# Moving the routing work, the first expert blocks and the first loads of a fused attention and expert kernel

## The chip, the cores and the metric

The kernel runs on one core of one Trainium2 chip. The metric is the device time of one execution in microseconds (us); smaller is better. A core has five engines that run side by side and wait for one another through semaphores: PE (matrix products, with PEld for its weight loads), DVE (vector), ACT (scalar functions), POOL (GpSimd) and SP (which here only issues transfers). Each engine works through its own list of instructions strictly in the order in which the program gives them. So the place of an instruction in the program text matters: what stands behind a waiting instruction on the same engine waits too.

## The reference

The first part is attention with random features. For each of 8 batches and 8 heads, with 576 rows of 64 values:

```python
proj = np.einsum('bhsd,md->bhsm', x, omega)                  # x is q or k; 128 features
phi = np.concatenate([np.cos(proj), np.sin(proj)], -1) / np.sqrt(m)
kv = np.einsum('bhsm,bhsd->bhmd', k_p, v);  z = np.sum(k_p, axis=2)
out = np.einsum('bhsm,bhmd->bhsd', q_p, kv) / np.einsum('bhsm,bhm->bhs', q_p, z)[..., None]
```

The heads of a row are put side by side: 4608 rows of 512 values. The second part sends each row to one of 8 experts:

```python
xn = x / (np.linalg.norm(x, axis=-1, keepdims=True) + 1e-06)  # en: the same of expert_emb
logits = xn @ en.T / tau;  expert_idx = np.argmax(logits, axis=1)
gate_w = softmax(logits)[np.arange(N), expert_idx]
out[mask] = gate_w[mask, None] * (np.maximum(x[mask] @ w1[e], 0) @ w2[e])   # mask: rows of expert e
```

## The kernel before

The attention runs in 32 steps; a step works on two heads of one batch. The steps are software-pipelined: step n makes the features of pair n, finishes pair n - 1 and prepares pair n + 1. One turn of the loop, cut to what is spoken of below (`nx` is true while another step follows):

```python
for n in range(NS + 1):                       # NS = 32; the turn n = NS finishes the last pair
    if n < NS - 2: load_v(n + 1)
    if n > 0: kv_copy(n - 1)                  # DVE
    if n > 1: to_rows(n - 2); sums(n - 2)     # POOL: rows to fp16, logits of the heads added up
    ...                                       # store_rows (SP), one 512 KB piece of expert weights (POOL)
    if n == NS - 1: gather(0)                 # POOL: 128 rows by index, the first expert block
    if n < NS:
        proj_q(n, ...)                        # PE, L233 and L241
        fold(n, "k"); whole_turns(n, "q"); wave(n, "si", "k")    # DVE, ACT, ACT
        zsum(n, 0)                            # POOL, L282 to L285
    route_first(n)                            # DVE: routing of the first two groups of batches
    if n == NS: turn_x(0, "act"); gather(3); hidden(0, "act")
    if n > 0:
        kv_turn(n - 1)                        # PE, L316 and L324; L324 reads the sums of zsum
        kv_out(n - 1)                         # DVE, L334: PSUM to the tile kv
    if nx: proj_k(n + 1); whole_turns(n + 1, "k")                # PE L221, ACT L254
    if n < NS: frac(n, "q"); wave(n, "co", "k"); zsum(n, 1)
    ...                                       # gather(1), square sums, frac(n + 1, "k")
    if n > 0: num(n - 1)                      # PE, L349, 72 matmuls; reads kv
    if n == NS: turn_x(1, "act")
    if n < NS: fold(n, "q")
    if nx: turns(n); copy_k(n); copy_q(n); load_kq(n + 1)        # PE L185
    route_pe(n)
    if n < NS: kv_products(n); wave(n, "si", "q"); wave(n, "co", "q")   # PE L295
    if n > 0: norm(n - 1)
    route_pool(n)                             # POOL: square roots of the norms, L724
    if n == NS - 1: gather(2)
```

The routing goes in two parts. The first covers groups 0 and 1 of the four groups of two batches and lies in the steps, so that 11 expert blocks can begin before the second part is known. The steps are counted from n0 = 10 and n1 = 18:

```python
elif n == n0 + 6: r1["g0"] = gates(0, 1, r1["rt", 0][0], ar1)     # step 16
elif n == n0 + 7: gates2(0, 1, *r1["g0"]); store_gates(0, 1)
m = n - n1
...
elif m == 2: scan(); square_rows(GRP1 - 1)                         # step 20
elif m == 8: row_hot(oh1, r1["lo"], 0, 6); choose(GRP1)            # step 26
elif m == 9: row_hot(oh1, r1["lo"], 6, 12); r1["g1"] = gates(1, 2, ...)
elif m == 10: row_hot(oh1, r1["lo"], 12, S1); block_experts(0, K1, False, r1["a"])
elif m == 12: gates2(1, 2, *r1["g1"]); store_gates(1, 2)
elif m == 13: square_rows(GRP1); choose2(GRP1)                     # step 31

def gates(g0, g1, rn, ar):                    # the weight of the chosen expert, first half
    nc.vector.tensor_tensor(sh, lsq[...], bc(lmax[...]), ALU.subtract)    # L732
    nc.vector.tensor_scalar(rn, rn, 1e-6, None, ALU.add)                  # L733; rn comes from POOL's root
    nc.vector.reciprocal(rn, rn)                                          # L734
    nc.vector.tensor_tensor(sh, sh, bc(rn, shp, 2), ALU.mult)             # L735
    nc.scalar.activation(sh, sh, AF.Tanh, scale=0.5)                      # L736, ACT
```

Then come the expert blocks of 128 rows, 40 that are always run and 3 behind a branch:

```python
def block(j, end):
    if j + 1 < end: hidden(j + 1, "act")      # PE L848, 32 matmuls; ACT
    route_second_pe(j)                        # rank at j = 2, invert at j = 7
    if j < end - 2: turn_x(j + 2, "act")      # PE L806 transposes; ACT copies
    route_second(j)                           # DVE; at j = 0 also root: POOL, 18 columns
    if j + 4 < NBLK: gather(j + 4)            # POOL
    result(j)                                 # PE L869, 8 matmuls; ACT; scatter of the rows (POOL, L886)
for j in range(LAST): block(j, LAST)          # LAST = 40
nb = nc.values_load(nblk[0:1, 0:1], ...)
with tc.If(nb > LAST): ...                    # the three further blocks
```

At the start the tile `kq` holds one pair's q and k; `load_kq(0)` comes after the transposes that free it.

Of the kernel before, what the change touches and what calls it, by code (L numbers as in the profile page):

```python
# [28 lines left out]
def kernel(  # L29
# [12 lines left out]
    nc = tc.nc  # L42
# [72 lines left out]
    eblk = persist.tile([1, NBLK], I32)  # L115
    nblk = persist.tile([1, 1], I32)
# [12 lines left out]
    pm = persist.tile([P, SG], FP32)  # L129
# [4 lines left out]
    with tc.tile_pool(name="psA", bufs=1, space=PSUM) as psA, tc.tile_pool(  # L134
# [5 lines left out]
        nm2 = ps[:, 6 * 512 :].rearrange("p (a w) -> p a w", a=2)  # L140

# [17 lines left out]
        ROUTED = tuple(range(n1 + 1, n1 + 13))  # L159


        def load_kq(m):
# [4 lines left out]
            t = pa.tile([P, 2 * NCH, 64], FP32, tag="kq", name="kq", bufs=1)  # L167
# [209 lines left out]
        def to_rows(n):  # L377
            b, i = steps[n]
            if i % 2 == 0:
                xrow[b, i // 2] = pa.tile([P, NCH, 2, 64], FP16, tag="xb", name="xb")  # L380
            nc.gpsimd.tensor_copy(xrow[b, i // 2][:, :, i % 2], st[n]["xa"][:, 0:NCH, 0:64])
# [18 lines left out]
        def square_rows(g):  # L400
            s0 = g * SG
            for par in range(2):
# [3 lines left out]
                nc.vector.tensor_copy(t[here, :, NPAIR:], t[there, :, 0:NPAIR])  # L406
                nc.vector.tensor_reduce(
# [3 lines left out]
        def sums(n):  # L411
            b, i = steps[n]
            src = st[n]["xa"][:, 0:NCH, 64 : 64 + E]
            if i == 0:
                lacc[b] = pa.tile([P, NCH, E], FP32, tag="la", name="la", bufs=3)
                nc.gpsimd.tensor_copy(lacc[b], src)
            else:
                nc.gpsimd.tensor_tensor(lacc[b], lacc[b], src, ALU.add)
# [25 lines left out]
        load_kq(-1)  # L444
        load_v(0)
        make_identity(nc, ident)
        nc.vector.memset(zmask, 0.0)
        nc.vector.memset(pio2, PI_2)
        nc.vector.memset(zmask[0:64, 0:1], 1.0)
# [47 lines left out]
        copy_k(-1)  # L497
        copy_q(-1)
        frac(0, "k")
        load_kq(0)  # L500
# [50 lines left out]
        def choose(g):  # L551
# [4 lines left out]
            nc.vector.tensor_copy(l0, a0[64:P])  # L556
            nc.vector.tensor_copy(l1, a1[0:64])
            nc.vector.tensor_tensor(l0, l0, a0[0:64], ALU.add)
            nc.vector.tensor_tensor(l1, l1, a1[64:P], ALU.add)
            nc.vector.tensor_reduce(lmax[:, s0 : s0 + SG], lg, axis=AX.X, op=ALU.max)  # L560

        def choose2(g):
# [3 lines left out]
            nc.vector.tensor_tensor(sel, lg, bc(mx, [P, SG, E], 2), ALU.is_equal)  # L566
            nc.vector.tensor_tensor(sel, sel, bc(pref, [P, SG, E], 1), ALU.mult)
            nc.vector.tensor_reduce(pm, sel, axis=AX.X, op=ALU.max)
            nc.vector.tensor_tensor(
# [9 lines left out]
        def scan():  # L579
            nc.vector.tensor_tensor_scan(flat(cumx), flat(keep), flat(eq), 0.0, ALU.mult, ALU.add)  # L580
# [9 lines left out]
        def before(dst, src, ar):  # L590

            t = ar.take(E * E).rearrange("p (a b) -> p a b", b=E)
            nc.vector.tensor_tensor(t, bc(src, [P, E, E], 1), tri, ALU.mult)
            nc.vector.tensor_reduce(dst.unsqueeze(2), t, axis=AX.X, op=ALU.add)

        def whole(dst, src, shift, mid=None):
            mid = dst if mid is None else mid
            nc.vector.tensor_scalar(mid, src, 1.0 / P, shift, ALU.mult, ALU.add)
            nc.vector.tensor_scalar(dst, mid, CMAGIC, CMAGIC, ALU.add, ALU.subtract)

        def starts1(rk, ns, ar):
            nc.vector.tensor_copy(sm[:, T0], rk[:, :, ns])
# [3 lines left out]
        def starts1b():  # L606
            nc.vector.tensor_scalar(sm[:, LIM], sm[:, FB], float(P), None, ALU.mult)
            nc.vector.tensor_scalar(sm[:, OFF1], sm[:, B1], float(P), None, ALU.mult)
            nc.vector.memset(sm[:, DOFF], BIG)

        def starts2(rk, ns, ar):
            nc.vector.tensor_copy(sm[:, T0], rk[:, :, ns])
            whole(sm[:, T1], sm[:, T0], 0.49609375)
            nc.vector.tensor_tensor(sm[:, T1], sm[:, T1], sm[:, FB], ALU.subtract)
            before(sm[:, ST2], sm[:, T1], ar)
            nb1 = sm[:, 8, 0:1]
            nc.vector.tensor_tensor(nb1, sm[:, B1, E - 1 : E], sm[:, FB, E - 1 : E], ALU.add)
            nc.vector.tensor_tensor(sm[:, ST2], sm[:, ST2], nb1.to_broadcast([P, E]), ALU.add)
            nc.vector.tensor_tensor(sm[:, T0], sm[:, ST2], sm[:, FB], ALU.subtract)
# [574 lines left out]
```

## Time and profile before

The median time is 497.8 us, of three executions from 496.01 to 497.95. The profiled execution spans 492.0 us.

| engine | busy us | share of the span |
|---|---|---|
| PE (matmuls) | 462.8 | 94% |
| PEld (weight loads) | 389.2 | 79% |
| POOL | 366.9 | 75% |
| ACT | 356.2 | 72% |
| DVE | 299.8 | 61% |

A line of the timeline gives the start and the duration in us, the engine, the line of the program, the operation and its tiles as out<-in, and in brackets how long the engine had stood idle and what ended that. A line of the chain of waits gives start, duration, engine, tile and line. The windows give, for a stretch of time, how long each engine was busy in it, the clock that PE was granted (1.00 is full) and the share of time in which the transfer engines worked.

### The profile page before, as it was taken

The page shows a single profiled execution, that of the slowest core. Times are in us where ns is not written, and L with a number is a line of the kernel's source. Part 1 is how long each engine was busy: PE and PEld are TensorE (multiplying, and loading weights), DVE is VectorE, ACT ScalarE, POOL GpSimd, SP SyncE. Part 2 cuts the span into 40 slices and gives each one's busy share as a digit, 9 for nine tenths or more (in the row PEclk, how much of TensorE's full clock was granted, in tenths as well). Part 3 has the DMA queues.
Part 4 walks back from the last instruction along what each step waited for, and adds up shares of the span by engine and source line. Part 5 has one row for each costly group of instructions (what it writes and reads, how often), then busy time and mean ns, then how long its engine had stood idle before and what let it go on. Part 6 is the DMA issues. An engine that isn't in the chain of part 4 may idle for free.

```text
span 492.0 us, 18747 instructions
## 1 busy us (share of the span) xinstructions
PE 462.8 (94%) x7924; PEld 389.2 (79%) x7924; DVE 299.8 (61%) x518; ACT 356.2 (72%) x473; POOL 366.9 (75%) x472
## 2 busy tenths in 40 slices
PE   8899999999999798999999999779999999999991
PEld 7788898898898687888888888566777777777770
DVE  4689888799888798898888788728930000000000
ACT  3787887887887587989887989725666666666661
POOL 3698888889899877889999788946765555554551
PEclk9999999999999899999998999989999999999997
DMA  4588798897777677977877779612433223232220
GB/s 123 143 175 161 182 169 166 184 172 158 182 157 153 133 146 185 161 163 159 173 140 161 167 152 170 101 41 68 120 104 103 97 88 106 82 119 89 83 81 20
DMA packets 57652, 65.63 MB, mean 133 GB/s; under 512 B 29397, under 2 KB 37589, under 8 KB 57568
## 3 DMA queue, kind: packets, MB, share of 16 engines
q0 software_dynamic: 18064, 30.96, 32.1%
q1 hardware_dynamic: 39104, 32.95, 26.6%
q8 instruction: 65, 1.06, 0.9%
q10 hardware_dynamic: 400, 0.49, 0.3%
q14 instruction: 19, 0.16, 0.1%
HBM read 67.90 MB, written 15.22 MB: 169 GB/s over the span
## 4 chain that ended last, share of the span: by engine, by line
PE 64%; POOL 13%; DVE 8%; DMA 5%; ACT 4%; issue 4%; SPq 1%; POOLq 0%; ACTq 0%; DVEq 0%
PE ps L848 13%; PE ps L869 12%; PE ps L349 12%; PE ps L295 8%; PE ps L185 5%; PE ps L221 4%; POOL zt L282 4%; PE ps L233 3%; POOL zs L284 2%; POOL zt L283 2%; POOL zs L285 2%; DMA kq<-in_k_dram 2%; PE ps L806 2%; PE ps L324 2%; DMA kq<-in_q_dram 1%
## 5 line engine op out<-in xcount | busy, mean ns | idle before, releaser
L349 PE MATMUL ps<-kv,siq 128*64 128x73 f32 x1152 | 79.4, 234 | 6.4 <-DVE kv L334 6.2
L848 PEld LDWEIGHTS <-w_sb 128*128 x1280 | 76.1, 99 | 10.6 <-issue 1.6
L848 PE MATMUL ps<-kq,w_sb 128*128 128x128 f16 x1280 | 79.3, 221 | 1.4 <-ACT kq L798 1.4
L349 PE MATMUL ps<-kv,coq 128*64 128x73 f32 x1152 | 77.9, 231 | 0.0
L869 PE MATMUL ps<-w_sb,cok 128*128 x320 | 75.4, 379 | 0.2 <-issue 0.2
L349 PEld LDWEIGHTS ps<-kv,siq 128*64 128x64 f32 x1152 | 64.0, 140 | 10.5 <-ACT sik L271 3.8
L349 PEld LDWEIGHTS ps<-kv,coq 128*64 128x64 f32 x1152 | 64.6, 141 | 0.0
L282 POOL TENSOR_TENSOR zt<-sik 128x512 f32<-128x512 f32 x32 | 41.0, 1281 | 25.2 <-ACT sik L271 25.0
L767 POOL DMA_INDIRECT xin_all<-rf_x,prm x43 | 45.7, 1062 | 15.4 <-PE ps L806 9.6
L869 PEld LDWEIGHTS <-cok 128*128 128x128 f16 x320 | 29.7, 98 | 28.9 <-issue 0.4
L283 POOL TENSOR_TENSOR zt<-zt 128x256 f32<-128x256 f32 x64 | 48.6, 759 | 5.0
L258 DVE SCALAR_TENSOR_TENSOR sik<-sik,ps 128x1152 f32<-128x1152 f32 x32 | 43.2, 1349 | 3.7 <-ACT sik L254 3.7
L208 ACT ACTIVATE qT<-ps 128x512 f32<-128x512 f32 x32 | 19.1, 596 | 35.6 <-DVE kT L199 35.6
L282 POOL TENSOR_TENSOR zt<-cok 128x512 f32<-128x512 f32 x32 | 43.9, 1373 | 0.8 <-ACT cok L271 0.8
L221 PE MATMUL ps<-omT,kT 64*128 64x128 f32 x576 | 44.0, 283 | 0.3 <-DVE kT L202 0.3
L258 DVE SCALAR_TENSOR_TENSOR siq<-siq,ps 128x1152 f32<-128x1152 f32 x32 | 43.0, 1344 | 1.8 <-ACT siq L254 1.8
L185 PE MATMUL ps<-ident,kq 128*128 128x128 f32 x288 | 38.4, 279 | 2.8 <-DMA kq<-in_k_dram 2.3
L295 PE MATMUL ps<-sik,v 64*64 64x128 f32 x612 | 37.4, 272 | 3.4 <-issue 3.4
L886 POOL DMA_INDIRECT out_dram<-siq,prm x20 | 22.3, 1117 | 23.6 <-ACT siq L885 22.3
L271 ACT ACTIVATE coq<-coq,consts 128x1152 f32<-128x1152 f32 x32 | 39.9, 1248 | 0.0
L271 ACT ACTIVATE cok<-cok,consts 128x1152 f32<-128x1152 f32 x32 | 39.9, 1248 | 0.0
L254 ACT ACTIVATE sik<-ps 128x1152 f32<-128x1152 f32 x32 | 36.2, 1132 | 4.8 <-PE ps L221 2.9
(213 smaller groups left out, 1158.9 us busy)
## 6 DMA issues: line engine op xcount, KB each, us to landing
w_sb<-in_moe_w_dram POOLq DMA_DIRECT2D x32, 512.0 KB, 6.6
kq<-in_q_dram SPq DMA_DIRECT2D x63, 144.0 KB, 3.7
kq<-in_k_dram SPq DMA_DIRECT2D x63, 144.0 KB, 3.9
v<-in_v_dram SPq DMA_DIRECT2D x34, 144.0 KB, 3.9
rf_x<-xb SPq DMA_DIRECT2D x32, 144.0 KB, 7.8
xin_all<-in_v_dram SPq DMA_DIRECT2D x30, 144.0 KB, 4.3
xin_all<-rf_x,prm POOLq DMA_INDIRECT x43, 2.9
out_dram<-sik,prm POOLq DMA_INDIRECT x20, 2.8
```

The source lines that it names most:

```text
L185: nc.tensor.transpose(qreg[:, j * P : j * P + P], t[:, j * P : j * P + P], ident)
L221: nc.tensor.matmul(kreg[:, s * P : s * P + P], lhsT=t[r0 : r0 + 64, j * P : j * P + P], rhs=omT[r0 : r0 + 64], start=True, stop=True,)
L254: nc.scalar.activation(si, REG[nm], AF.Copy, bias=CMAGIC, scale=1.0)
L258: nc.vector.scalar_tensor_tensor(out=si, in0=si, scalar=CMAGIC, in1=REG[nm], op0=ALU.subtract, op1=ALU.subtract)
L271: nc.scalar.activation(t, t, AF.Sin, bias=pio2 if which == "co" else 0.0, scale=-TWO_PI * SINSC)
L282: nc.gpsimd.tensor_tensor(zt, t[:, 0:4], t[:, 4:8], ALU.add)
L283: nc.gpsimd.tensor_tensor(zt[:, 0:2], zt[:, 0:2], zt[:, 2:4], ALU.add)
L295: nc.tensor.matmul(kreg[64 * half : 64 * half + 64, 512 * hh : 512 * hh + P], lhsT=d["v"][r0 : r0 + 64, c], rhs=ph[r0 : r0 + 64, s * P : s ...
L349: nc.tensor.matmul(nm2[r0 : r0 + 64, a, (c - c0) * W : (c - c0) * W + W], lhsT=ph[:, s * P + r0 : s * P + r0 + 64], rhs=d["kv"][:, half, h ...
L767: ins = nc.gpsimd.indirect_dma_start(out=t, out_offset=None, in_=x_rows[:], in_offset=bass.IndirectOffsetOnAxis(ap=prm[:, j : j + 1], axis=0),
L848: nc.tensor.matmul(h_ps[:, f * P : f * P + P], lhsT=weights(k), rhs=d["xT"][:, c * P : c * P + P], start=(c == 0), stop=(c == 3),)
L869: nc.tensor.matmul(y_ps, lhsT=d["hT"][:, c * P : c * P + P], rhs=weights(NW1 + NW2 * (j % 2) + c), start=(c == 0), stop=(c == NW2 - 1),)
```

## The change

It has six parts.

1. **Loads at once.** The q and k of the first pair get their own place (in the room of a late expert's weights), so the next pair's load need not wait. The order of the first copies is changed too, and each piece of expert weights is issued one step earlier from step 2 on.
2. **Gates once, in place.** The weights of groups 0 and 1 are computed together, in steps 24 to 30, in the tile that holds the logits; the computation in steps 16 and 17 goes.
3. **Routing work held.** The DVE instructions of `route_first` are kept back, let out up to an estimated 0.9 us before `kv_out`, and the rest behind it; in the last step all of it comes behind.
4. **First block woven into the last step.** `turn_x(0)` moves ahead of the last `kv_products`, and the gathers 1 to 3 behind the sums on POOL. Rows of two late steps are converted on ACT.
5. **Second routing.** The rank is taken at block 1, the inversion at block 6; the roots move to blocks 3 and 4 in pieces, the gates to block 5.
6. **Last scatters.** The scatters of blocks 38 and 39 stand behind the branch.

The diff, cut to its core (`...` marks the cuts; `nc.vector` became `rv` throughout the routing helpers):

```diff
+        held = []
+        hold = [False]
+        def do(f, *a, **k):
+            if hold[0]:
+                held.append((f, a, k))
+            else:
+                f(*a, **k)
...
+        rv, ra = Engine(nc.vector), Engine(nc.scalar)
+        def release(budget):
+            spent = 0.0
+            while held:
+                ...                             # width: elements of the output in a partition
+                cost = 0.2 + width / 960.0
+                if spent + cost / 2 > budget:
+                    return
+                spent += cost
+                held.pop(0)
+                f(*a, **k)
...
-            t = pa.tile([P, 2 * NCH, 64], FP32, tag="kq", name="kq", bufs=1)
+            if m == -1:
+                t = (w2_sb[:, E - 2] ... )
+            else:
+                t = pa.tile([P, 2 * NCH, 64], FP32, tag="kq", name="kq", bufs=1)
...
         load_kq(-1)
+        load_kq(0)
         load_v(0)
...
         turns(-1)
-        copy_k(-1)
         copy_q(-1)
         frac(0, "k")
-        load_kq(0)
+        fold(0, "k")
+        copy_k(-1)
...
+            if NS - 3 <= n < NS - 1:            # in to_rows
+                nc.scalar.activation(dst, src, AF.Copy)
+            else:
+                nc.gpsimd.tensor_copy(dst, src)
...
-        def gates(g0, g1, rn, ar):
...
+        def gates_a(g0, g1):
+            rv.tensor_tensor(sh, sh, bc(lmax[:, s0:s1], shp, 2), ALU.subtract)
+        def gates_b(g0, g1):
+            rv.tensor_scalar(rn, rn, 1e-6, None, ALU.add)
+            rv.reciprocal(rn, rn)
+            rv.tensor_tensor(sh, sh, bc(rn, [P, s1 - s0, E], 2), ALU.mult)
+            ra.activation(sh, sh, AF.Tanh, scale=0.5)
+        def gates_c(g0, g1):                    # 1 - sh, reciprocal
+        def gates_d(g0, g1):                    # sum, times 2, minus E, reciprocal
...
-            elif n == n0 + 6:
-                r1["g0"] = gates(0, 1, r1["rt", 0][0], ar1)
-            elif n == n0 + 7:
-                gates2(0, 1, *r1["g0"])
-                store_gates(0, 1)
...                                             # gates_a at m == 6
             elif m == 8:
                 row_hot(oh1, r1["lo"], 0, 6)
-                choose(GRP1)
+                gates_b(0, GRP1)
...                                             # gates_c at m == 11
             elif m == 12:
-                gates2(1, 2, *r1["g1"])
-                store_gates(1, 2)
+                gates_d(0, GRP1)
+                store_gates(0, GRP1)
+                choose(GRP1)
...
-        WORDER = [None, 0, 1, *range(2, 4 * E - 4), ...]
+        WORDER = [*range(4 * E - 4), ...]
...
-            for piece in () if n == 0 else WORDER[n + 1 : n + 2] if n > 1 else WORDER[1:3]:
+            for piece in () if n == 0 else WORDER[n + 1 : n + 2] if n > 2 else WORDER[2 * n - 2 : 2 * n]:
...
+            hold[0] = True
             route_first(n)
+            hold[0] = False
+            release(0.9 if n < NS - 1 else 0.0)
             if n == NS:
-                turn_x(0, "act")
-                gather(3)
                 hidden(0, "act")
             if n > 0:
                 kv_turn(n - 1)
                 kv_out(n - 1)
+            release(100.0)
...
-            if n == NS:
-                turn_x(1, "act")
+            if n >= NS - 1:
+                turn_x(n + 1 - NS, "act")
...
             if n == NS - 1:
+                gather(1)
                 gather(2)
+                gather(3)
...
-            if j == 2:
-                r2["ps"] = rank(NSLOT, bank(6))
-            elif j == 7:
+            if j == 1:
+                r2["ps"] = rank(NSLOT, bank(6 - 4 * (j % 2)))
+            elif j == 6:
                 r2["inv"] = invert(
...
-                root(GRP1, *r2["rt"], 0, (NGRP - GRP1) * SG)        # block 0
...
+            if j in (3, 4):                     # block
+                for a in range(GRP1 * SG + SG * (j - 3), GRP1 * SG + SG * (j - 2), 3):
+                    root(a, a + 3)
             result(j)
+            if not LAST - 2 <= j < LAST:
+                scatter(j)
...
+        scatter(LAST - 2)
+        scatter(LAST - 1)
```

## The prediction

> **What bounds the kernel now.** I read the page first, then the chain of waits, PE's list of waits, and the timeline at each place where the chain leaves PE. PE is busy for 94% of the span, and it leads the chain:
>
> ```profile
> PE 462.8 (94%) x7924; PEld 389.2 (79%) x7924; DVE 299.8 (61%) x518; ACT 356.2 (72%) x473; POOL 366.9 (75%) x472
> ...
> 41.48 1.31 PE ps L221 x18
> ...
> 50.71 1.31 PE ps L221 x18
> ...
> 344.89 1.79 PE ps L848 x32
> 346.90 1.73 PE ps L869 x8
> 348.62 1.79 PE ps L848 x32
> ```
>
> The lines below the first are of the chain. Two `proj_k` (L221) start 50.71 - 41.48 = 9.23 us apart, and two blocks 348.62 - 344.89 = 3.73. In both stretches PE works without a gap, and the change takes no matmul away. So only what a step takes beyond 9.23 us, a block beyond 3.73, and the two ends can be won. From PE's timeline, the starts of `proj_q` (L233) show which steps are long: step 16 takes 13.72 us (159.64 to 173.36; 4.49 too many), 18 takes 10.92 (1.69), 20 takes 9.92 (0.69), 21 9.48 (0.25), 26 11.99 (2.76), 28 10.21 (0.98). The other small ones add 1.9: 12.7 us in all. PE's own waits name the releasers (total, times, longest):
>
> ```profile
> PE ps L349 <- DVE kv L334: 6.2, 6, 2.6
> PE ps L295 <- issue: 3.4, 1, 3.4
> PE ps L185 <- DMA kq<-in_k_dram: 2.3, 2, 1.6
> PE ps L324 <- POOL zs L285: 1.7, 5, 0.9
> PE ps L848 <- ACT kq L798: 1.4, 2, 0.7
> ```
>
> The first is `num` waiting for `kv_out` while DVE still does routing. The timelines of DVE and PE in step 16 and in step 31:
>
> ```profile
> 162.72 0.63 DVE L733 TENSOR_SCALAR w_sb<-w_sb 128x9 f32<-128x9 f32 x1 [1.31 <-POOL w_sb L724]
> ...
> 163.64 2.08 DVE L735 TENSOR_TENSOR w_sb<-w_sb 128x72 f32<-128x72 f32 x1
> 165.64 0.45 DVE L334 COPY kv<-ps 128x292 f32<-128x292 f32 x1
> ...
> 166.24 0.51 PE L349 MATMUL ps<-kv,siq 128*64 128x73 f32 x4 [2.63 <-DVE kv L334]
> ...
> 313.42 0.60 DVE L334 COPY kv<-ps 128x292 f32<-128x292 f32 x1
> ```
>
> The gates of step 16 wait 1.31 us for a root on POOL and then lose 2.08 us in one small product, and `kv_out` stands behind them. In step 31 the copy waits behind eight instructions of m = 13; PE has its last matmul before it at 312.29 and starts `num` at 314.17.
>
> **What the Trainium skill says.** "TensorE: Matmul & The Clock Gate", section "What's actually happening": PE's clock falls to half after an idle window of about 3.4 us, and the window runs freely. The trace agrees on the half clock and its length (three stretches of 3.4 us before the end), not on the idleness: an idle time of 0.92 us in step 26 was enough. The windows show the loss:
>
> ```profile
> 160.00:173.00 13.00, 10.16 (x181) 9.25 (x181) 10.48 (x15) 7.15 (x10) 10.38 (x15) 0.87 0.64 130
> ...
> 291.00:300.00 9.00, 9.00 (x190) 7.96 (x185) 7.75 (x14) 7.76 (x10) 7.65 (x11) 1.00 0.86 170
> ```
>
> The columns are the stretch, its length, PE, PEld, DVE, ACT and POOL busy, the granted clock, the DMA share and GB/s. The 72 matmuls of `num` took 3.93 us in step 16 against 2.44 in the chain's quiet steps: 1.5 us lost on top of the wait, and 1.7 in step 26 (4.13).
>
> "SBUF — State Buffer", section "SBUF: two separate sides": DVE with two inputs there and POOL share a pair of ports, and one blocks the other for a whole instruction. The trace agrees: the 72-element product above took 2.08 us where `choose2`'s took 0.23, and a `row_hot` on DVE (1.20 us from 261.36) stretched POOL's L285 from 0.46 to 1.05.
>
> "Runtime: NRT & Kernel Launch", section "Instruction fetch mechanics": engines fetch instructions by DMA in blocks of 16 KiB. The trace has 65 packets of 16 KB in the instruction queue. Of these one is late. In step 31 PE stops for 3.40 us in the midst of `kv_products`, waiting for nothing ("issue"), from 318.02. A fetch starts only at 319.22, after some 150 instructions more than are usual at a fetch, while the last weight piece (issued at 312.40) and gather(0) fill the transfer engines. I take that as its cause, though the trace doesn't prove it.
>
> **The change part by part.**
>
> Gates out of step 16: 2.63 wait + 1.5 slow clock + 0.21 of POOL's wait, about 4.3 of the 4.49 go. The later gates stand behind `kv_out`. Tanh may hold ACT for some 0.5 us in step 26, which I expect to be hidden.
>
> Held routing: `kv_out` comes earlier. PE's idle times before L349 in steps 20, 21 and 28 are 0.48, 0.18 and 0.47: 1.1 us won. Behind `kv_out` there is room, since DVE must end `frac` of q before `turns`: 1.3 us of `proj_k` and 2.4 of `num`, 3.7, less 0.5 for the copy and 1.35 for `frac`, leave 1.9 us, and the held rests are 0.5 to 1.9 us (instructions of 0.2 to 0.3, `block_hot` 1.5).
>
> Step 26: `row_hot` is let out before `kv_out` still (its estimate is 0.2 + 768/960 = 1.0, half of it under 0.9), so POOL is blocked as before. But the roots come a step earlier, so POOL is less behind. Whether the clock falls depends on where the window lies. I take half of 2.76: 1.4.
>
> Step 18 waited 1.65 us for a load of k whose issue on SP took 2.24 us. Nothing in the change aims at it: 0.
>
> Step 31 and the first blocks: without routing before the copy, `num` still waits about 0.6 us (copy 0.46 and two semaphores, with no `proj_k` to fill), so of 1.88 some 1.3 go. No weight piece is left in step 31, so gather(0) stands behind nothing and lands about 3 us after its issue (2.9 is the page's median). The late fetch should also go: 3.4 and the slow clock after it (`hidden(0)` took 3.23 us, not 1.95: 1.3), 4.7 together; at a chance of 0.65 that is 3.1. `turn_x(0)` before `kv_products` hides one of the two waits of 0.69 for ACT's xT (L848 in the list above): 0.7.
>
> Blocks: block 2 begins its L869 4.19 us after the last instead of 2.66 (1.53 more), since gather(4) stood behind POOL's root of 18 columns, 3.26 us. Of this the rank's own matmuls remain (0.41): 1.1 won. The inversion's 1.05 us merely move from block 7 to block 6. But six roots of three columns cost about 0.95 each (0.88 to 1.05 in the steps), 5.7 us on POOL in blocks 3 and 4. There DVE's `block_hot` and `row_hot` already stretch scatters and gathers from 1.03 to about 2.1 us. POOL has 3.73 - 2.1 = 1.6 us free in a block, and a gather about 3.5 us until its block wants it. And DVE must end `row_hot` by block 6 with, by my sum, 1.4 us to spare. I charge 1.3 us for both.
>
> Start: the second pair's load no longer waits until 9.79, but `turns(0)` at 16.22 was released by DVE's `frac`, not by this load. `proj_q(0)` waits longer (both copies from PSUM must end: about 12.05, not 11.55), then `whole_turns(0, "q")` comes before a wave and gains about 0.8. Net 0.3 won. The second pair of pieces in step 2 costs POOL 0.9 us (1.77 for two), with slack of some 0.7 a step: zsum late in step 3, 0.4 lost.
>
> Tail: POOL loads the block count (0.75 us) earlier, but its last scatter waits for ACT anyway, and the 5.5 us of the final drain remain: 0.2.
>
> Sum of gains: 4.3 + 1.1 + 1.4 + 1.3 + 3.1 + 0.7 + 1.1 + 0.3 + 0.2 = 13.5. Losses: 1.3 + 0.4 = 1.7. Net 11.8, so 497.8 - 11.8 = 486.0 us (I carry the span's difference over one to one).
>
> **The rivals.** First, the stall for instructions stays or moves: the same number of matmuls must be fetched, and the last stretch now has more transfers at once. Then 3.1 is not won, nor the slow clock behind it, and the time is about 489. For it: it is one event in a trace, and I only infer its cause. Against it: no other fetch is late so, and the weight piece is gone.
>
> Second, POOL and DVE become the bound in blocks 3 to 7: a gather late by 2 to 3 us, or PE waiting for `row_hot` at block 6. For it: both share ports and the roots are put where DVE works most. Gather 11 must also wait for the stores of the gates, which now leave after block 5 (the page's landing time for them is 8.1 us). The time would be 488 to 490. Against: the gathers run two blocks ahead.
>
> Third, the held work comes back as late `frac`, `wave` and `turns` in several steps, half a us each: 488. Against it stands the 1.9 us of room; step 31, with 2.3 us of held work, has the least, but there no `turns` follows.
>
> Fourth, all goes well and step 26 loses its slow clock too: 481 to 483.
>
> **Range and chances.** The middle is 486.0. The uncertain items are the late fetch (0 or 4.7), the slow clocks (1.5 each) and the blocks (0 to 3), so 481.0 to 491.0 should hold it 8 times in 10. Faster by over 2% means below 487.8, which lies a little above the middle: 0.66. Within 2%: 0.31. Slower by over 2%: 0.03, for nothing is added to PE.
>
> **What would show it.** Right: step 16 takes about 9.3 us; the wait of L349 for L334 falls from 6.2 to under 2 us; no "issue" wait of 3 us near the last `kv_products`; from the last `proj_q` (L233 of step 31) to the start of `hidden(1)`, 22 us become about 15.5; blocks keep 3.73 us with two exceptions of 0.4 and 1.05. Wrong: new waits of L185 for DVE's `frac`, of L806 for gathers in blocks 5 to 9, of the inversion (L674) for DVE, or a slow clock in other steps.

## The result, and the profile after

The changed kernel takes 485.14 us (median of four executions, 484.44 to 485.76) against 497.88 us before (496.01 to 498.03): the ratio is 0.9752, 95% interval 0.9725 to 0.978. The prediction said 486.0.

The time is nearly the predicted one, but the sum behind it is not. The two traces, cut at the same instructions of PE (us; "step 0" is the first `proj_q`, the tail runs from PE's last product to the end of the span):

| stretch | before | after | gain | predicted |
|---|---|---|---|---|
| start to step 1 | 20.40 | 22.23 | -1.83 | 0.3 |
| steps 1 to 30 | 289.60 | 283.23 | 6.37 | 6.4 |
| step 31 to `hidden(1)` | 21.99 | 16.53 | 5.45 | 5.1 |
| blocks, `hidden(1)` to `hidden(39)` | 144.56 | 148.16 | -3.6 | -0.2 |
| tail | 10.09 | 8.34 | 1.75 | 0.2 |
| sum | | | 8.14 | 11.8 |

What the table leaves out, from `hidden(39)` to PE's last product, takes 5.4 us in both.

Two terms failed by 5.5 us, and two others made up 1.9 of it. The rest of the 12.74 us of the medians, 4.6, is not in these traces: the traced executions took 493.92 and 485.76 us, so that of before was 4 us quicker than its other executions and that of the changed kernel 0.6 slower.

PE's busy line of the page after:

```profile
PE 462.3 (96%) x7924; PEld 387.8 (80%) x7924; DVE 298.8 (62%) x506; ACT 357.8 (74%) x475; POOL 371.5 (77%) x472
```

PE's list of waits after (total, times, longest):

```profile
PE ps L850 <- DMA xin_all<-rf_x,prm: 4.0, 2, 2.9
PE ps L363 <- POOL zs L324: 2.1, 6, 0.7
...
PE ps L719 <- DVE sik L297: 0.7, 1, 0.7
...
PE ps L388 <- DVE kv L373: 0.6, 1, 0.6
```

The lines have moved by about 40: L388 is `num` (L349 before), L363 the sums of z (L324), L334 `kv_products`, L850 `turn_x`, L719 the inversion, L811 a gather, L941 a scatter. As predicted, the wait for kv has fallen from 6.2 to 0.6 us and the stop of 3.4 us for "issue" is gone. PE's busy time is as before (462.3 and 462.8). New at the head is `turn_x` waiting for gathers, which the prediction had named as a sign of its being wrong.

In step 16 DVE now goes straight to the copy of kv and on to `frac`. Its timeline there:

```profile
164.40 0.46 DVE L373 COPY kv<-ps 128x292 f32<-128x292 f32 x1 [1.32 <-PE ps L363]
164.78 1.34 DVE L297 SCALAR_TENSOR_TENSOR siq<-siq,ps 128x1152 f32<-128x1152 f32 x1
```

Step 16 takes 9.57 us instead of 13.72, and the full clock is kept (1.00 from 160 to 173 us). In step 31 (PE's timeline) `num` waits 0.65 us instead of 1.88, and the transposes wait 1.01 us for gather(0), which landed 4.4 us after its issue at 307.51, not 3 us:

```profile
308.39 0.35 PE L388 MATMUL ps<-kv,siq 128*64 128x73 f32 x4 [0.65 <-DVE kv L373]
...
311.91 0.40 PE L850 MATMUL ps<-ident,xin_all 128*128 128x128 f16 x4 [1.01 <-DMA xin_all<-rf_x,prm]
```

The blocks hold the loss. POOL's timeline in blocks 3 to 6:

```profile
337.85 4.92 POOL L762 TENSOR_TENSOR lsq<-lsq,pmh 128x3 f32<-128x3 f32 x3
342.95 2.52 POOL L941 DMA_INDIRECT out_dram<-siq,prm  x1 [0.18 <-issue]
345.77 1.03 POOL L811 DMA_INDIRECT xin_all<-rf_x,prm  x1 [0.30 <-PE ps L893]
346.83 2.55 POOL L762 TENSOR_TENSOR lsq<-lsq,pmh 128x3 f32<-128x3 f32 x3
```

PE's timeline at block 6:

```profile
346.97 0.69 PE L719 MATMUL ps<-ar,ohq 128*128 128x64 bf16 x18
350.60 0.40 PE L850 MATMUL ps<-ident,xin_all 128*128 128x128 f16 x4 [2.94 <-DMA xin_all<-rf_x,prm]
350.93 2.62 PE L914 MATMUL ps<-w_sb,cok 128*128 x8
```

The first three roots (3 columns each) take 4.92 us together and the scatter behind them 2.52, so gather(8) is issued only at 345.77 and lands at 350.56. PE stands for 2.94 us, and 1.3 us after that its clock falls: eight products take 2.62 us where 1.89 are usual.

### The profile page after: what moved, and what is told of

It is laid out like the page before. It is cut to its first block, busy times and chain, and to the rows that moved or that the text cites. A ratio compares the mean times of both kernels' runs of the same rounds, so it can differ in the third digit from the quotient of the medians.

```text
span 483.9 us, 18742 instructions
## 1 busy us (share of the span) xinstructions
PE 462.3 (96%) x7924; PEld 387.8 (80%) x7924; DVE 298.8 (62%) x506; ACT 357.8 (74%) x475; POOL 371.5 (77%) x472
## 4 chain that ended last, share of the span: by engine, by line
PE 54%; POOL 18%; DVE 12%; DMA 7%; ACT 5%; issue 3%; POOLq 0%; SPq 0%; ACTq 0%
PE ps L893 13%; PE ps L914 12%; PE ps L388 8%; PE ps L334 6%; POOL zt L321 5%; PE ps L260 4%; PE ps L224 3%; POOL zt L322 3%; POOL zs L324 3%; POOL zs L323 3%; DMA out_dram<-sik,prm 3%; PE ps L272 3%; DVE sik L297 2%; DMA kq<-in_q_dram 2%; DVE siq L297 2%
## 5 line engine op out<-in xcount | busy, mean ns | idle before, releaser
L388 PE MATMUL ps<-kv,siq 128*64 128x73 f32 x1152 | 76.4, 229 | 1.4 <-DVE kv L373 0.6
L388 PE MATMUL ps<-kv,coq 128*64 128x73 f32 x1152 | 74.9, 226 | 0.0
L388 PEld LDWEIGHTS ps<-kv,siq 128*64 128x64 f32 x1152 | 60.5, 135 | 5.3 <-ACT xb L422 0.7
L388 PEld LDWEIGHTS ps<-kv,coq 128*64 128x64 f32 x1152 | 61.1, 137 | 0.0
L811 POOL DMA_INDIRECT xin_all<-rf_x,prm x43 | 45.5, 1057 | 17.0 <-PE ps L850 9.6
L260 PE MATMUL ps<-omT,kT 64*128 64x128 f32 x576 | 45.1, 288 | 0.0
L321 POOL TENSOR_TENSOR zt<-cok 128x512 f32<-128x512 f32 x32 | 42.8, 1339 | 0.0
L310 ACT ACTIVATE siq<-siq 128x1152 f32<-128x1152 f32 x32 | 37.1, 1160 | 4.3 <-DVE coq L303 4.3
L293 ACT ACTIVATE siq<-ps 128x1152 f32<-128x1152 f32 x32 | 35.9, 1123 | 5.8 <-PE ps L280 5.8
L260 PEld LDWEIGHTS ps<-omT,kT 64*128 64x128 f32 x576 | 39.1, 192 | 1.1 <-issue 0.5
```

Source lines behind the costliest of these rows:

```text
L260: nc.tensor.matmul(kreg[:, s * P : s * P + P], lhsT=t[r0 : r0 + 64, j * P : j * P + P], rhs=omT[r0 : r0 + 64], start=True, stop=True,)
L293: nc.scalar.activation(si, REG[nm], AF.Copy, bias=CMAGIC, scale=1.0)
L310: nc.scalar.activation(t, t, AF.Sin, bias=pio2 if which == "co" else 0.0, scale=-TWO_PI * SINSC)
L321: nc.gpsimd.tensor_tensor(zt, t[:, 0:4], t[:, 4:8], ALU.add)
L388: nc.tensor.matmul(nm2[r0 : r0 + 64, a, (c - c0) * W : (c - c0) * W + W], lhsT=ph[:, s * P + r0 : s * P + r0 + 64], rhs=d["kv"][:, half, h ...
L811: ins = nc.gpsimd.indirect_dma_start(out=t, out_offset=None, in_=x_rows[:], in_offset=bass.IndirectOffsetOnAxis(ap=prm[:, j : j + 1], axis=0),
```

## The experiments

There were three series. The first two ran on chips on which both kernels need 4.39 us for a block (not 3.73) from about block 12 on: ACT takes up the second half of `hidden` 1.0 us after PE's last product there (0.1 us in the first trace), and PE then waits some 0.5 us for ACT in each block. The third ran on a chip like that of the first result. Times are therefore compared within a series. The medians and ranges contain some executions at a lower granted clock, above all of the kernel before; the ratios leave these out. Against the kernel before none of the ratios below is clear of 2%, so the theories are judged by the traces, of which there is one for each run. Steps are compared across them: where nothing special falls into a step, it takes 9.23 us on all.

### First series: before 522.99 us (516.81 to 534.88)

**before_again**: the kernel before, unchanged.

> The kernel before, traced once more. The trace I predicted from spans 492.0 us, while the timed executions took 496.0 to 498.0, so the gain of 12.7 us in time is only 8.1 us from trace to trace. If the first trace was a lucky execution, the second spans 494 to 496 us, and the step in which the 2 to 4 us more lie shows whether it is a transfer (a step like 18 that waits for k) or a slow clock. If instead the trace is always shorter than the timed executions, the second one spans 492 again with the same list of long steps, and the missing 4.6 us can't be seen in traces.

522.59 us in one execution. Step 16 takes 13.69 us, `num` waits 1.87 us for kv in step 31, and PE stops for 3.7 us in `kv_products` of the last step again. So these three belong to the kernel and not to one execution. Step 18 now takes 14.99 us, with a wait of 4.1 us for the load of k (1.65 in the first trace): how large that wait is differs from one execution to the next. And step 26, which took 11.99 us in the first trace with the half clock in it, takes 10.37 here.

**weights_old**: the changed kernel with the pieces of expert weights issued as before, so that one is issued in step 31 again, and step 2 issues one piece and not two.

```diff
-        WORDER = [*range(4 * E - 4), ...]
+        WORDER = [None, 0, 1, *range(2, 4 * E - 4), ...]
...
-            for piece in () if n == 0 else WORDER[n + 1 : n + 2] if n > 2 else WORDER[2 * n - 2 : 2 * n]:
+            for piece in () if n == 0 else WORDER[n + 1 : n + 2] if n > 1 else WORDER[1:3]:
```

> The changed kernel with the old order of the expert weights: the last 512 KB piece is issued in step 31 again, ahead of gather(0), and step 2 issues one piece, not two. Late-fetch theory: the transfer of that piece is what held up the instructions of PE and gather(0), so a stop of about 3 us comes back in the last kv_products or before turn_x(0), gather(0) lands 7 to 8 us after its issue instead of 4.4, and the time is 488 to 490 us. Rival (the stop came from where the code lay, and the reorder of turn_x and the gathers cured it): no stop, 485 us, at most 1 us from the changed kernel. The wait of 0.31 us in step 1 and 0.26 in step 3 may shrink.

518.75 us, ratio 0.9943 (0.9905 to 0.998). PE's timeline at `turn_x(0)` in this run:

```profile
321.70 0.61 PE L850 MATMUL ps<-ident,xin_all 128*128 128x128 f16 x4 [5.54 <-DMA xin_all<-rf_x,prm]
```

The same in the next run, root_moved, which issues no piece there:

```profile
314.07 0.40 PE L850 MATMUL ps<-ident,xin_all 128*128 128x128 f16 x4 [2.02 <-DMA xin_all<-rf_x,prm]
```

With the piece of weights POOL issues gather(0) at 313.58, and it lands 8.1 us later; PE waits 5.54 us, and in that wait the clock falls to half. Without the piece (root_moved) it lands 5.2 us after its issue and PE waits 2.02 us. The stretch from step 31 to `hidden(1)` is 23.38 us against 19.25 and 20.20 in the two neighbours. So taking the piece out of step 31 is worth 3 to 4 us there. But the stop for "issue" did not come back in step 31; one of 2.5 us came in step 19.

**root_moved**: the changed kernel with the roots of the second routing as two operations of 9 columns, in blocks 1 and 3.

```diff
-            if j in (3, 4): ... root(a, a + 3)          # six of 3 columns
+            if j in (1, 3): ... root(s0, s0 + SG)       # two of 9 columns
```

> The changed kernel with the square roots of the second part as two instructions of nine columns, in blocks 1 and 3, in place of six of three columns in blocks 3 and 4. Theory (POOL is overfilled in blocks 3 and 4 by six roots that share ports with row_hot, which makes gather(8) leave 2.9 us late, and the idle time brings a slow clock): the wait of 2.9 us and the slow clock after it go, the blocks take 3 to 5 us less, 481 to 482 us. Rival (gather(8) is late because of row_hot alone, or the gates' Tanh on ACT waits for DVE and holds ACT): the wait stays at 2 us or more, and the time stays above 484.

511.79 us, ratio 0.979 (0.9683 to 0.9897). No wait of `turn_x` is left in the blocks. They take 168.67 us against 170.18 and 170.00 in the two neighbours with six roots, 1.4 us less (the theory asked for 3 to 5), although PE stops for 2.4 us in all for "issue" at the inversion here.

**load_old**: the changed kernel with `load_kq(0)` at its old place; the copies stay in their new order.

> The changed kernel with the second pair's load issued where it was before, after the first copies; its place and the order of the copies stay as changed. In the changed kernel step 0 starts at 13.84 us instead of 11.55. Theory (the 288 KB more that are asked for at once delay omega and the first k and q, and PE, left waiting, runs its first products at half clock, 2.50 us for the 18 of proj_k instead of 1.38): step 0 starts at 12.0 to 12.3 again and the time falls by 1.5 to 2 us. Rival (the new order of the copies is what costs, since proj_q must wait for copy_k, which now comes last on DVE): step 0 starts at 13.2 or later and the time falls by less than 0.7.

511.69 us, ratio 0.977 (0.9673 to 0.9867). Step 0 begins at 14.14 us, between before_again (13.22) and the two runs with the early load (14.46 and 14.91); `proj_q(0)` waits 1.13 us for the copy of k. The order of the copies already costs time. The load by itself can't be told from the clock here: the first 18 products of `proj_k` took 1.93 us in this run, 2.4 and 2.5 in the other two and 2.5 in before_again.

### Second series: before 522.55 us (516.3 to 534.89)

**after_again**: the changed kernel.

> The changed kernel itself, so that the other three stand beside it on one chip. All theories: a ratio to the kernel before of about 0.975 (0.97 to 0.98). In the trace, steps 1 to 30 take 283 to 284 us, the stretch from step 31 to hidden(1) 16.5 to 19 us, step 28 again about 2 us too long. If the long blocks of the first trace belong to the kernel (POOL's roots behind and under VectorE's row_hot hold gather(8) back) then PE waits again at turn_x(8) of block 6 for 2 to 3 us; if they were that execution's slow clock alone, no block is over 1 us longer than its neighbours.

508.83 us, ratio 0.9777 (0.9654 to 0.9899). Steps 1 to 30 take 283.19 us (283.23 in the first trace), step 28 again 11.56. Here PE does not wait for gather(8), since a block takes longer on this chip. Against before_again the steps gain 9.2 us, more than the 6.37 of the first pair, because of the longer wait for k in step 18 of before_again.

**late16**: the kernel before, with the gates of step 16 behind `kv_out`, and nothing else.

```diff
-            route_first(n)
+            if n != n0 + 6: route_first(n)
...
             kv_out(n - 1)
+            if n == n0 + 6: route_first(n)
```

> The kernel before with one move alone: the gates of group 0 in step 16 are issued behind kv_out(15) in place of ahead of it. Theory (step 16 lost its 4.3 us because these operations stood ahead of kv on VectorE and waited there for the root): step 16 is 9.3 to 10 us long in place of 13.7, and steps 1 to 30 lose 3.5 to 4.5 us; the time falls by 3 to 4.5 us, ratio 0.991 to 0.994. Rival (their length counts wherever they stand, and only doing them once and in place helps): step 16 is still 11.5 us or longer, the wait has moved from kv to turns or frac, and the time falls by less than 2 us.

518.62 us, ratio 0.9969 (0.9937 to 1.0001). Here the rival won. Step 16 takes 12.03 us, and step 17 9.91: 21.94 together, against 23.09 before and 19.17 after. DVE, ACT and PE in step 16, from the timeline:

```profile
164.17 0.46 DVE L334 COPY kv<-ps 128x292 f32<-128x292 f32 x1 [1.32 <-PE ps L324]
...
165.76 1.82 DVE L735 TENSOR_TENSOR w_sb<-w_sb 128x72 f32<-128x72 f32 x1
...
166.18 1.30 POOL L282 TENSOR_TENSOR zt<-sik 128x512 f32<-128x512 f32 x1
...
167.50 1.34 DVE L258 SCALAR_TENSOR_TENSOR siq<-siq,ps 128x1152 f32<-128x1152 f32 x1
...
167.61 0.26 ACT L736 ACTIVATE w_sb<-w_sb 128x72 f32<-128x72 f32 x1 [2.47 <-DVE w_sb L735]
...
168.90 1.20 PE L185 MATMUL ps<-ident,kq 128*128 128x128 f32 x9 [1.01 <-DVE siq L258]
```

The copy is now on time, but `frac` (L258) starts 3.33 us after it instead of 0.38 us as in the changed kernel; the product L735 alone lasts 1.82 us and ends with POOL's (167.58 and 167.48). ACT waits 2.47 us at Tanh and carries the delay to the next wave, and PE waits for both: 1.01 us at `turns` and 0.72 at `kv_products`. So the new place alone brings 23.09 - 21.94 = 1.15 of the 3.92 us. The other 2.77 need the computation to be gone from there.

**no_hold**: the changed kernel without the holding of routing instructions.

```diff
-            hold[0] = True
```

> The changed kernel with routing operations put straight into their step instead of being held until after kv_out. Theory (the held list saves the waits of PE for kv that VectorE's routing work caused in steps 20, 21, 28 and 31): those waits come back, kv_out or num waits 0.3 to 1.5 us each there, steps 1 to 30 take 1.0 to 2.5 us more than in the changed kernel, and step 28's 2.3 us stays or shrinks only by 1. Rival (the held work only moves the wait to frac, wave and the turns later in the step, as step 28 suggests): steps 1 to 30 are within 0.5 us of the changed kernel, step 28 loses its 2.3 us and other steps gain as much.

513.73 us, ratio 0.9863 (0.9738 to 0.9989). The waits for kv are back in steps 20, 21, 26, 28, 29 and 30: 0.56, 0.22, 0.59, 0.39, 0.42 and 0.37, together 2.55 us. But step 28 takes 10.12 us instead of 11.56, and steps 1 to 30 lose only 0.4 us. In step 31 the wait for kv is 1.70 us instead of 0.64. Of the 4.9 us between the medians this explains 1.5; in the trace there is also a stop of DVE, 4.48 us ahead of the last copy of kv, for which the profile names no cause within the kernel.

**best1**: the changed kernel with load and first copies in their old order, the roots of root_moved, and `block_experts` one step sooner.

```diff
...
             elif m == 9: row_hot(oh1, r1["lo"], 6, 12)
+                block_experts(0, K1, False, r1["a"])    # was at m == 10
```

> The changed kernel with three repairs: the loads and copies of the start as in the kernel before, the roots of the second routing as two operations of 9 columns in blocks 1 and 3 in place of six of 3 columns in blocks 3 and 4, and block_experts(0, K1) one step sooner, in step 27. Theory (start, POOL in blocks 3 to 7 and step 28 are three separate losses): q0 comes 0.5 to 2 us sooner, no wait of PE for gather(8), step 28 under 1 us over the common length; 3 to 6 us less than the changed kernel on the same chip. Rival for the blocks (the slow clock and not POOL): the blocks take as long as in the changed kernel; rival for step 28 (the other held work, not block_experts): step 28 keeps its 2.3 us or step 27 takes it over. With both rivals the gain is 0.5 to 1.5 us.

508.83 us, ratio 0.9767 (0.9641 to 0.9894): the changed kernel's own time. The blocks gain 1.56 us (168.73 against 170.29). Step 28 loses most of its excess (9.67 us), but step 27 takes 11.01 us: the delay went along with `block_experts`. The start gains nothing (step 1 at 22.93; the first products ran at half clock), and a stop of 1.9 us for "issue" fell into step 21.

### Third series: before 499.95 us (492.4 to 502.13)

**after_third**: the changed kernel.

> The changed kernel once more, as the neighbour on the same chip of the three below. All theories: step 28 11.56 us, steps 1 to 30 283.2 us where no late stop of PE falls into them, tail 8.34 us. Theory (a stop of PE that the profile calls issue follows the transfer traffic and not a place in the code): the chance that this profile has one in steps 17 to 21 or in step 31 is about a half; rival (it belongs to a variant's code): none, as in the two profiles of this kernel so far.

485.44 us (484.33 to 488.43), ratio 0.9834 (0.975 to 0.9918). The blocks take 148.19 us, as in the first trace, with the same wait of 2.9 us for gather(8). No stop for "issue". But step 28 takes 9.66 us here, with the same code, and that shows where about half of its 2.3 us comes from. DVE and POOL in step 28, from the timeline of the changed kernel's first trace:

```profile
279.10 1.61 DVE L174 TENSOR_SCALAR eblk<-w_sb 1x11 int32<-1x11 f32 x1
279.38 1.29 POOL L321 TENSOR_TENSOR zt<-sik 128x512 f32<-128x512 f32 x1
```

And from that of this run:

```profile
278.71 0.16 DVE L174 TENSOR_SCALAR eblk<-w_sb 1x11 int32<-1x11 f32 x1
...
279.37 1.30 POOL L321 TENSOR_TENSOR zt<-sik 128x512 f32<-128x512 f32 x1
```

The last instruction of `block_experts`, 11 numbers in one partition, takes 0.16 us if it starts 0.66 us ahead of POOL's product, and 1.61 us if it starts 0.28 us ahead: then it ends with POOL's product (280.71 and 280.67). That delays `frac` and, through it, the copy of k and the inversion. Of the eleven profiles of the changed kernel and its variants, eight have it at 1.60 or 1.61 us, with a lead of 0.27 or 0.28, and three (no_hold, after_third, best2) at 0.16, with a lead of 0.65 or 0.66; there is nothing between. In seven of the eight, step 28 takes 11.56 us; in the eighth, best1, the instruction lies in step 27 and that step is the long one. In the three, step 28 takes 9.7 to 10.1. The other half is PE's wait of 0.7 us for POOL's sums of z, which `row_hot` stretches; in this run it fell into step 27 (10.05 us). Steps 27 and 28 together are 2.34 us too long in the first trace and 1.25 here, so the meeting of the two instructions costs about 1.1 us, from this one pair of traces.

**best2**: the changed kernel with the roots of root_moved, and without holding in step 28 alone.

```diff
...
-            hold[0] = True
+            hold[0] = n != n1 + 10
...
```

> The changed kernel with two repairs: the roots of the second routing as two operations of 9 columns in blocks 1 and 3, and no holding in step 28 alone. Theory (in step 28 the held rows of one-hots reach the wave and the turns too late, everywhere else holding pays): step 28 is 10.0 to 10.3 us in place of 11.56, the other steps are those of the changed kernel, and blocks 1 to 39 take 1.5 to 1.8 us less than in the changed kernel on the same chip; in all 2.5 to 3.5 us less, ratio to the kernel before 0.970 to 0.974. Rival (step 28's wait is passed on): step 28 shrinks but step 29 or 30 grows by more than 0.8 us, and the time is within 1.5 us of the changed kernel.

481.85 us (480.32 to 484.92), ratio 0.9743 (0.9638 to 0.9847): 3.6 us less than its neighbour in the medians, and the quickest version of this study. The blocks take 145.17 us against 148.19. The two traces as a whole are only 1.1 us apart (481.4 and 482.5), since in this one the start, steps 1 to 30 and the tail take 0.7, 0.8 and 0.4 us longer. PE's timeline at blocks 6 and 9:

```profile
347.07 0.69 PE L719 MATMUL ps<-ar,ohq 128*128 128x64 bf16 x18
347.59 0.39 PE L850 MATMUL ps<-ident,xin_all 128*128 128x128 f16 x4
...
360.58 0.40 PE L850 MATMUL ps<-ident,xin_all 128*128 128x128 f16 x4 [1.61 <-DMA xin_all<-rf_x,prm]
```

POOL's timeline in blocks 1 to 7:

```profile
329.52 1.86 POOL L762 TENSOR_TENSOR lsq<-lsq,pmh 128x9 f32<-128x9 f32 x1
...
337.43 2.03 POOL L762 TENSOR_TENSOR lsq<-lsq,pmh 128x9 f32<-128x9 f32 x1
...
341.64 2.15 POOL L811 DMA_INDIRECT xin_all<-rf_x,prm  x1 [0.30 <-issue]
...
356.10 1.03 POOL L811 DMA_INDIRECT xin_all<-rf_x,prm  x1 [4.31 <-PE ps L850]
```

Two roots take 3.9 us of POOL instead of 7.5 for six. Gather(8) is issued at 341.64 instead of 345.77, and `turn_x(8)` follows the inversion without a gap. In block 3 both kernels compute the roots of nine columns at the same place, ahead of the scatter and of gather(8): here in one operation of 2.03 us, in the changed kernel in three of 4.92 us together. That is 2.9 of the 4.1 us by which gather(8) is earlier. The other nine columns, here in block 1, are in block 4 in the changed kernel and stand behind gather(8) there. With the wait for gather(8) gone, another one shows: gather(11) is issued only at 356.10, after POOL has stood idle for 4.31 us, and `turn_x(11)` in block 9 waits 1.61 us for it. By the program this gather must wait for the stores of the gates; the view names PE's L850 instead, and other releasers in other runs, so that cause is argued and not shown. Step 28 takes the expected 10.12 us, but since its neighbour's took 9.66, this run shows no gain from not holding there.

**tail_old**: the changed kernel with the last two scatters ahead of the branch.

```diff
-            if not LAST - 2 <= j < LAST:
-                scatter(j)
+            scatter(j)
...
-        scatter(LAST - 2)
-        scatter(LAST - 1)
```

> The changed kernel with the last two scatters at their old places ahead of the branch. Theory (the tail fell by 1.75 us because the 1.5 us that GpSimd spends at the branch after an indirect transfer now lies ahead of the last scatters, under VectorE's and PE's end): the tail from PE's last product to the end of the span is 9.8 to 10.1 us in place of 8.34. Rival (the later place of y or the order of the last copies makes the tail short): the tail stays at 8.3 to 8.8 us. In both the rest of the trace is that of the changed kernel.

487.71 us (487.32 to 489.44), ratio 0.987 (0.9798 to 0.9942). The tail is 10.07 us, as in the kernel before. One instruction of the branch, from the view by line of this run (duration in ns as least, median and longest; first and last start in us):

```profile
L1204 POOLq INC_SWDGE_SEM  x1: 1526/1526/1526, 477.8 to 477.8; - x1
```

The same in the changed kernel:

```profile
L1205 POOLq INC_SWDGE_SEM  x1: 1491/1491/1491, 472.5 to 472.5; - x1
```

At the branch POOL's sequencer spends 1.5 us on this instruction. At the old place it comes after the last scatter and ahead of the final drain, so it lengthens the end. At the new place it comes while PE still works on the last blocks. The final drain then ends 5.5 us after the last scatter; in tail_old it ends 5.5 us after this instruction and 7.2 us after the scatter.

**start_old**: the changed kernel with the start as before (load, copies and the order in step 0).

> The changed kernel with the start as before: load_kq(0) behind the first copies, copy of k ahead of copy of q, fold and wave of step 0 in their old order. Theory (the order of the copies, not the early load, makes PE wait at the first proj_q): no wait of 0.7 to 1.1 us for the copy of k there, and step 1 begins at 22.0 to 22.3 us if the first proj_k takes 2.5 us, and at 21.4 to 21.7 us if it takes 1.9 us, which is 0.5 to 1 us before the changed kernel with the same proj_k. Rival (the clock of the first products alone sets the start): step 1 begins within 0.3 us of the changed kernel with the same proj_k. Either way the whole time falls by at most 1 us, which is inside its interval.

485.84 us (484.06 to 492.66), ratio 0.9822 (0.9724 to 0.9919). PE's timeline at the start, in the changed kernel's first trace:

```profile
4.96 0.45 PE L527 MATMUL ps<-ident,w_sb 128*128 128x128 f32 x1 [0.30 <-DMA w_sb<-in_omega_dram]
...
7.20 2.50 PE L260 MATMUL ps<-omT,kT 64*128 64x128 f32 x18
...
13.84 0.70 PE L272 MATMUL ps<-qT,omT 64*128 64x512 f32 x2 [0.68 <-DVE kT L238]
```

And in this run:

```profile
4.62 0.47 PE L526 MATMUL ps<-ident,w_sb 128*128 128x128 f32 x1
...
6.72 1.38 PE L260 MATMUL ps<-omT,kT 64*128 64x128 f32 x18 [0.26 <-DVE kT L241]
...
11.63 1.13 PE L272 MATMUL ps<-qT,omT 64*128 64x512 f32 x4
```

Step 1 begins at 20.48 us, as before the change (20.40), and 1.25 us sooner than in after_third. Two things are undone: the wait for the copy of k, and the half clock. The clock goes with omega: in the two profiles in which PE did not wait for omega (before and start_old) the 18 products took 1.38 us; in the twelve in which it waited 0.14 to 1.34 us they took 1.93 to 2.50. The granted clock is full from 5.4 and 5.8 us in the two, and from 8.7 to 11.8 us in the twelve. On the other chips PE waited for omega with the old start too, so what delays omega is not only the early load. A gain in the time is not shown: the medians are 485.84 and 485.44, and step 28 was the long one here and the short one in after_third.

## Why the prediction was right, and where only its sum was

**Gates out of step 16**: predicted 4.3, measured 4.15 (4.49 to 0.34 us beyond 9.23). Right, but late16 shows that most of it comes from removing the work and not from its place behind `kv_out`.

**Held routing**: predicted 1.1. Steps 20 and 21 gave 0.57, and step 28 lost 1.36 more than before, most of it (1.1) by one instruction of `block_experts`. The room of 1.9 us was worked out from the lengths that DVE's instructions have alone, but one of 0.16 us can last as long as POOL's product. The section of the Trainium skill that the prediction cites ("SBUF — State Buffer", "SBUF: two separate sides") names, beside instructions with two inputs, those in a mode with two ports; the prediction took up only the first kind, and this instruction has one input. The trace agrees with an instruction that is blocked until the other ends (1.61 us instead of 0.16), though it had started 0.28 us before the other; no view shows its mode. This is the third rival, at one place. The waits that holding removed were there (2.55 us in no_hold).

**Step 26**: half of 2.76 was counted, all of it went. But the half clock in it belonged to that one execution: before_again and late16 take 10.37 and 10.35 us there, and 9.94 each in step 27. **Step 18**: nothing was counted, 1.69 went, without any wait for the load of k in the profile. "Nothing in the change aims at it" overlooked part 2: before, SP issues two stores of the gates in step 17, between the loads of one pair and of the next, and the change moves them to step 30, behind the last such load. Of the three profiles with the stores in step 17, two have the wait (1.65 and 4.11 us) and late16 has none; of the eleven without them, none has it. That the stores cause it was not tried alone. Steps 26 and 18 and the held routing cancel, so 6.37 against 6.4 is in part luck. The first steps cost the 0.4 that was charged to the second piece of weights (0.73 us too long in steps 1 and 3, 0.33 in step 2 before). But only the 0.26 of step 3 is that piece's, which is gone in weights_old; with the old start (start_old) steps 1 and 2 are as before, so their 0.14 belongs to the start.

**Step 31**: the wait for kv gave 1.24 of the 1.3. The late stop went in full, 4.7 instead of 4.7 times 0.65. `turn_x(0)` did not win its 0.7, since it now waits for gather(0), which takes 4.4 us to land and not 2.9. The first rival (the stop stays or moves) did not come in this trace. But the cause named for it, the weight piece together with gather(0), is not enough: in weights_old both are there and PE does not stop. All three profiles with the old last step have a stop of 3.4 to 3.7 us there; of the eleven with the new one, three have one of 1.9 to 2.5 us in steps 19 to 21, and one a stop of DVE in the last step. The packets in the traces support the reading as a late fetch: in all six stops of PE a 16 KB packet of the instruction queue starts 2.20 to 2.46 us before PE goes on. What makes the fetch late is left open.

**Blocks**: this is the step that failed: "I charge 1.3 us for both". It cost 4.9: from `hidden(7)` to `hidden(9)` the changed kernel takes 13.38 us, and two blocks of 3.74 with the inversion's 1.05 would be 8.53. The second rival came instead, with the wait of 2 to 3 us that it named. The six roots took 7.5 us and not 5.7: the last three cost 0.85 each, but the first three 4.92 beside DVE's one-hots. And the first three stand ahead of the scatter and of gather(8), so their length falls on one gather and is not spread over the free 1.6 us of each block. Best2 does nine columns there in one operation and gets 3.0 of the 3.6 us back; what the move of the other nine to block 1 adds was not tried alone.

**Start**: predicted 0.3 won, 1.8 lost. The copy of k now ends last and `proj_q(0)` waits 0.68 us for it; and the first products run at half clock (2.50 instead of 1.38 us), which the prediction didn't consider.

**Tail**: predicted 0.2, measured 1.75. The prediction saw the count's load move, but not the 1.5 us at the branch that lay between the last scatter and the drain.

So 486.0 was met because losses of 5.5 us that were not foreseen stand beside gains of 1.9 that were not foreseen, and because the profile of before was one of its quicker executions. Why its other executions are 4 us slower was not tried; the wait for k in step 18, which is 1.65 and 4.11 us in two profiles with the old step 17 and absent in the third, is one candidate.

## What to carry to other kernels

Moving small vector work behind a critical copy pays only if nothing near its new place is tight as well; see what it will run beside, and above all whether GpSimd then holds the ports that both share. Join many small GpSimd operations into few larger ones and keep them away from the transfers that GpSimd itself must issue: it is the transfer behind them that PE waits for. And when a sum of terms meets the time, compare it with the trace stretch by stretch, or two errors pass for knowledge.

## What the runs showed of the hardware

- An instruction of VectorE on 11 numbers took 1.61 us instead of 0.16 when it started 0.28 us ahead of a product on GpSimd, and ended within 0.05 us of it.
- The square root by power on GpSimd costs less per column in a larger operation: 0.85 us for 3 columns (1.6 in the mean of the three beside DVE's one-hots), 1.9 to 2.0 for 9, 3.26 for 18.
- At a branch behind indirect transfers GpSimd's sequencer spends 1.5 us on one instruction, and the final drain takes 5.5 us beyond what is last ahead of it.
- A gather of 128 rows took 8.1 us from issue to landing behind a 512 KB piece issued by the same engine, in before and in weights_old. Without the piece it took 4.4 us on the chip of before and 5.2 us on that of weights_old.
- The products after the wait for omega were slow already after a wait of 0.14 us (2.12 us for the 18, in after_third), and half clock followed the 2.94 us of block 6; after the 1.61 us of block 9 in best2 the clock stayed full.
- In six of the 14 profiles PE stopped for 1.9 to 3.7 us without a wait that the profile shows, and went on 2.20 to 2.46 us after a 16 KB packet of the instruction queue had started.
